# Windowed attention into a gated unit: one four-bank score tile against two two-bank tiles

## The chip, the cores and the metric

The kernel runs on one core of one Trainium2 chip. The metric is the device time of one execution in microseconds; the time before is the median of three executions. The profile is of one further execution, taken by the hardware profiler. Engine names are those of the profile: PE is TensorE, with PEld for its weight loads, DVE is VectorE, ACT is ScalarE, POOL is GpSimd, SP is SyncE.

## The reference

Eight batches of 576 positions go through an attention of 8 heads with head size 64, and its result through a gated unit of width 512. Heads 0 to 3 see the last 32 positions; heads 4 to 7 see every fourth of the last 128.

```python
def _attn_ref(q, k, v):                      # each (8, 8, 576, 64) fp32
    scores = 1.0 / np.sqrt(64) * np.matmul(q, k.transpose(0, 1, 3, 2))
    rel = pos[:, None] - pos[None, :]
    mask_plain = (rel >= 0) & (rel < 32)                         # heads 0-3
    mask_dil = (rel >= 0) & (rel < 128) & (rel % 4 == 0)         # heads 4-7
    scores = np.where(masks, scores, -1e9)
    attn = np.exp(scores - max(scores)); attn = attn / (sum(attn) + 1e-9)
    return np.matmul(attn, v)

def _moe_ref(x, w_val, conv_w, w_out):       # x: (8, 576, 512)
    gate_pre = sum over k of conv_w[k] * (x shifted by 4 - k positions)   # 5 taps, causal
    gate = 1.0 / (1.0 + np.exp(-gate_pre))
    return (gate * (x @ w_val)) @ w_out      # fp32 out
```

## The kernel before

The work is cut into 32 steps, four to a batch. A step does two heads: steps 0 and 1 of a batch have plain windows, steps 2 and 3 dilated ones. Each step is done in two halves (`hf` 0 and 1). The program order is written by hand and kept on every engine (`manual_schedule`); the framework adds the semaphores between engines, and a new tile of a pool waits until the readers of the tile whose place it takes are done.

PSUM has eight banks of 2 KiB in each partition. The kernel divides them among three pools:

```python
    ps_tr = ctx.enter_context(tc.tile_pool(name="ps_tr", bufs=2, space=PSUM))    # transposes: 2 x 1 bank
    ps_sc = ctx.enter_context(tc.tile_pool(name="ps_sc", bufs=1, space=PSUM))    # scores: 1 x 4 banks
    ps_moe = ctx.enter_context(tc.tile_pool(name="ps_moe", bufs=2, space=PSUM))  # gated unit: 2 x 1 bank
```

A half step of attention: six score matmuls into two banks of the score tile, one exponential over both, a multiply by the 0/1 mask, six products with V. The V operand has a column of ones, so that each product brings its sum of weights along. The products go into the first of the half's two banks, over the scores.

```python
    def scores(i, hf):
        if hf == 0:
            st[(i, "ps")] = ps_sc.tile([128, 4, 512], FP32, name="ps_sc")
        ps = st[(i, "ps")][:, 2 * hf:2 * hf + 2, :]
        for n in range(3):
            for sl in range(2):
                ...
                nc.tensor.matmul(out=o, lhsT=lhsT, rhs=rhs, start=True, stop=True)       # L386
        ...
        nc.scalar.activation(out=e3, in_=ps[:, :, 0:HB], func=AF.Exp, scale=scale)       # L389

    def apply_mask(i, hf):
        ...
        nc.vector.tensor_tensor(out=e3, in0=e3, in1=m, op=ALU.mult)                      # L398

    def attn_v(i, hf):
        et, ps = st[(i, "et")], st[(i, "ps")]
        ...                                                        # 6 of:
                nc.tensor.matmul(                                                        # L416
                    out=ps[:, 2 * hf, x * AVS:x * AVS + D + 1],
                    lhsT=et[:, (2 * hf + sl) * HB + col:(2 * hf + sl) * HB + col + 128],
                    rhs=rhs, start=True, stop=True)

    def normalize(i):                                              # both halves at once
        ...
        nc.vector.reciprocal(out=rec[0:R], in_=av[:, :, :, D])                           # L428
        ...
        nc.vector.tensor_tensor(                                                         # L433
            out=dst, in0=av[:, :, :, 0:D],
            in1=rec[0:R, :, :, None].to_broadcast([R, 2, 6, D]), op=ALU.mult)
```

`trans_main` (L312) and `trans_rest` (L345) transpose the queries and keys of the next group of heads into a `ps_tr` tile, from which ScalarE and VectorE copy them out (L322 to L358). `trans_x` (L445 to L460) transposes the normalized output into `xT`. The gated unit takes `ps_moe` tiles: `conv` (L484, read by a tanh at L492), `val` (L499, read by the gating multiply into `y_all` at L505) and `out_tile` (L514, copied out at L519 and stored). One step puts them in this order:

```python
        scores(i, 0)
        scores(i, 1)
        if i > 0:
            trans_x(i - 1)
            ...
        if g + 1 < 2 * B:
            ...            # trans_main(g + 1, "k"), or trans_main(g + 1, "q") and trans_rest(g + 1)
        ...
        apply_mask(i, 0)
        ...
        pop_dense(0.5)     # val or out_tile, as a budget allows
        pop_conv(i)
        apply_mask(i, 1)
        ...
        attn_v(i, 0)
        pop_conv(i + 0.5)
        ...
        attn_v(i, 1)
        normalize(i)
        ...                # the first three steps: warming matmuls on junk data (L576)
        pop_dense(1.5)
```

Of the kernel before, what the change touches and what calls it, by code (L numbers as in the profile page):

```python
# [7 lines left out]
FP32 = mybir.dt.float32  # L8
BF16 = mybir.dt.bfloat16
I32 = mybir.dt.int32  # L10
AF = mybir.ActivationFunctionType
ALU = mybir.AluOpType
PSUM = bass.MemoryType.PSUM
# [10 lines left out]
def kernel(  # L24
# [11 lines left out]
    nc = tc.nc  # L36
# [29 lines left out]
    gate_pool = ctx.enter_context(tc.tile_pool(name="gate", bufs=16))  # L66
    out_pool = ctx.enter_context(tc.tile_pool(name="osb", bufs=4))

    ps_tr = ctx.enter_context(tc.tile_pool(name="ps_tr", bufs=2, space=PSUM))
    ps_sc = ctx.enter_context(tc.tile_pool(name="ps_sc", bufs=1, space=PSUM))  # L70
    ps_moe = ctx.enter_context(tc.tile_pool(name="ps_moe", bufs=2, space=PSUM))

    ctx.enter_context(tc.manual_schedule())

# [23 lines left out]
    conv_diag = consts.tile([128, NCH, K, 128], BF16, name="conv_diag")  # L98
    w_val_b = consts.tile([128, NCH, Dm], BF16, name="w_val_b")
    w_out_b = consts.tile([128, NCH, Dm], BF16, name="w_out_b")  # L100


    grp_tiles = {}
# [171 lines left out]
            out=mb, in0=mb, in1=same[:, :, None].to_broadcast([128, 2, TR]), op=ALU.mult)  # L275

    def setup_conv_w():
        ps = ps_moe.tile([128, 512], FP32, name="ps_moe")
        for c in range(NCH):
            nc.tensor.transpose(  # L280
                out=ps[:, c * 8:c * 8 + K], in_=conv_nat[:, c * 128:(c + 1) * 128],
                identity=ident5[0:K, 0:K],
            )
        nc.scalar.copy(
            out=conv_w_sb, in_=ps[:, 0:NCH * 8].rearrange("p (c e) -> p c e", c=NCH)[:, :, 0:K])
# [15 lines left out]
    def trans_main(g, name, pairs=(0, 1)):  # L301

        dil = g % 2
        t = grp_tiles[g]
        ps = ps_tr.tile([128, 2, RM], BF16, name="ps_tr")
        for z in pairs:
            for m in range(4):
                if not dil:
                    src = t[name + "b"][:, m, 2 * z:2 * z + 2, :]
                else:  # L310
                    src = hi_bf16(t[name][:, 2 * z + m // 2, 128 * (m % 2):128 * (m % 2) + 128])
                nc.tensor.transpose(out=ps[:, z, TM * m:TM * m + TM], in_=src, identity=ident)  # L312
        z0, z1 = pairs[0], pairs[-1] + 1
        if name == "q":
            if not dil:
                if "qT" not in t:
                    t["qT"] = qt_pool.tile([128, 2, DIL, T], BF16, name="qT")
                qd, qs = t["qT"][:, z0:z1, :, 0:TM], ps[:, z0:z1, :].rearrange("p z (r t) -> p z r t", r=DIL)
                if g == 0:
                    nc.vector.tensor_copy(qd, qs)  # L320
                else:
                    nc.scalar.copy(out=qd, in_=qs)  # L322
            else:
                t["qA"] = qt_pool.tile([128, 2 * RM], BF16, name="qA")
                nc.scalar.copy(out=t["qA"], in_=ps.rearrange("p z n -> p (z n)"))
        else:
            if not dil:
                t["kT"] = kTs[(g // 2) % NKT]
                nc.scalar.copy(
                    out=t["kT"][:, z0:z1, KOFF:KOFF + RM].rearrange("p z (t r) -> p z t r", r=DIL),  # L330
                    in_=ps[:, z0:z1, :].rearrange("p z (r t) -> p z t r", r=DIL))
            else:
                t["kA"] = qt_pool.tile([128, 2 * RM], BF16, name="kA")
                t["kB"] = qt_pool.tile([128, 4, 64, 2], BF16, name="kB")
                nc.scalar.copy(out=t["kA"], in_=ps.rearrange("p z n -> p (z n)"))
                nc.scalar.copy(
                    out=t["kB"][:, :, 0:TM - TB, :],
                    in_=ps.rearrange("p z (h w t) -> p (z h) t w", h=2, w=2)[:, :, TB:TM, :])

    def trans_rest(g):  # L340
        dil = g % 2
        t = grp_tiles[g]
        ps = ps_tr.tile([128, 2, RM], BF16, name="ps_tr")
        for z in range(2):
            nc.tensor.transpose(  # L345
                out=ps[:, 0, TM * z:TM * z + TM],
                in_=hi_bf16(t["rest"][:, 128 * z:128 * z + 128]), identity=ident)
        pv = ps[:, 0, 0:256].rearrange("p (z n) -> p z n", z=2)
        if not dil:
            nc.vector.tensor_copy(t["kT"][:, :, KOFF + RM:KOFF + S], pv[:, :, 0:64])  # L350
            nc.vector.tensor_copy(
                t["qT"][:, :, :, TM:T], pv[:, :, 64:128].rearrange("p z (t r) -> p z r t", r=DIL))
        else:
            t["qB"] = qt_pool.tile([128, 4, 2, TR], BF16, name="qB")
            nc.vector.tensor_copy(
                t["kB"][:, :, TM - TB:64, :],
                pv[:, :, 0:64].rearrange("p w (h t) -> p h t w", h=4))
            nc.vector.tensor_copy(  # L358
                t["qB"], pv[:, :, 64:128].rearrange("p w (h t) -> p h w t", h=4))
# [3 lines left out]
    def scores(i, hf):  # L363
        b, c, dil, g, a = pair_info(i)
        t = grp_tiles[g]
        if hf == 0:
            st[(i, "ps")] = ps_sc.tile([128, 4, 512], FP32, name="ps_sc")
        ps = st[(i, "ps")][:, 2 * hf:2 * hf + 2, :]
        for n in range(3):
            for sl in range(2):  # L370
                p0 = sl * D
                if not dil:
                    m = 3 * hf + n
                    o = ps[:, sl, 96 * n:96 * n + 96]
                    lhsT = t["kT"][p0:p0 + D, a // 2, 96 * m:96 * m + 128]
                    rhs = t["qT"][p0:p0 + D, a // 2, :, 24 * m:24 * m + 24]
                elif n < 2:
                    x = TM * (2 * (a + hf) + n)
                    o = ps[:, sl, TM * n:TM * n + TM]
                    lhsT = t["kA"][p0:p0 + D, x:x + TM]  # L380
                    rhs = t["qA"][p0:p0 + D, x:x + TM]
                else:
                    o = ps[:, sl, 2 * TM:HB]
                    lhsT = t["kB"][p0:p0 + D, a + hf, :, :]
                    rhs = t["qB"][p0:p0 + D, a + hf, :, :]
                nc.tensor.matmul(out=o, lhsT=lhsT, rhs=rhs, start=True, stop=True)  # L386
        et = ets[i % NET]
        e3 = et[:, 2 * hf * HB:2 * (hf + 1) * HB].rearrange("p (h n) -> p h n", h=2)
        nc.scalar.activation(out=e3, in_=ps[:, :, 0:HB], func=AF.Exp, scale=scale)  # L389
        st[(i, "et")] = et  # L390
# [8 lines left out]

    def attn_v(i, hf):  # L400
        b, c, dil, g, a = pair_info(i)
        et, ps = st[(i, "et")], st[(i, "ps")]
        for n in range(3):
            for sl in range(2):
                if not dil:
# [2 lines left out]
                else:  # L408
# [5 lines left out]

                x = 3 * sl + n if dil else 2 * n + sl
                nc.tensor.matmul(  # L416
                    out=ps[:, 2 * hf, x * AVS:x * AVS + D + 1],
                    lhsT=et[:, (2 * hf + sl) * HB + col:(2 * hf + sl) * HB + col + 128],
                    rhs=rhs, start=True, stop=True)

    def normalize(i):
        b, c, dil, g, a = pair_info(i)
        R = 128 if dil else 96
        xn = st[(i, "xn")] = xn_pool.tile([128, 2, 3, 2, D], BF16, name="xn")
        av = st[(i, "ps")][0:R].rearrange("p (f s) c -> p f s c", f=2)[:, :, 0, 0:6 * AVS].rearrange(
            "p f (x e) -> p f x e", x=6)
        rec = rec_pool.tile([128, 2, 6], FP32, name="rec")
        nc.vector.reciprocal(out=rec[0:R], in_=av[:, :, :, D])  # L428
        if dil:
            dst = xn[0:R].rearrange("p z n h d -> p h (z n) d")  # L430
        else:
            dst = xn[0:R].rearrange("p z n h d -> p z (n h) d")
        nc.vector.tensor_tensor(  # L433
            out=dst, in0=av[:, :, :, 0:D],
            in1=rec[0:R, :, :, None].to_broadcast([R, 2, 6, D]), op=ALU.mult)

    def trans_x(i):
        b, c, dil, g, a = pair_info(i)
        xn = st[(i, "xn")]
        px = ps_tr.tile([128, 2, RM], BF16, name="ps_tr").rearrange("p z n -> p (z n)")  # L440
        ps = px[:, 0:S]
        pr = ps.rearrange("p (r t) -> p r t", r=DIL)
        if not dil:
# [21 lines left out]

    def conv(b, c, G):
        xt = xTs[b % NXT]
        ps = ps_moe.tile([128, 512], FP32, name="ps_moe")
        r0 = 2 * G
        pieces = []  # L470
        for m in range(K):
# [22 lines left out]

    def val(b, c, G):
        xt = xTs[b % NXT]
        ps = ps_moe.tile([128, 512], FP32, name="ps_moe")
        for mc in range(NCH):
            nc.tensor.matmul(  # L499
                out=ps[:, 0:HB],  # L500
# [8 lines left out]
        )  # L509

    def out_tile(n):
        ps = ps_moe.tile([128, 512], FP32, name="ps_moe")
        for c in range(NCH):
            nc.tensor.matmul(  # L514
                out=ps, lhsT=y_all[:, c, 128 * n:128 * n + 128], rhs=w_out_b[:, c, :],
# [40 lines left out]
    def pop_conv(i):  # L556
        if convs and convs[0][0] < i:
            run(convs.pop(0)[1])
# [13 lines left out]

    def warm(n):
        for _ in range(n):
            ps = ps_moe.tile([128, 512], FP32, name="ps_moe")
            nc.tensor.matmul(out=ps, lhsT=junk[:, 0:128], rhs=junk, start=True, stop=True)  # L576

    warm(8)
# [7 lines left out]
    for i in range(NP):  # L586
# [35 lines left out]
        if i < 3:  # L622
            warm(2)
        attn_v(i, 0)
        pop_conv(i + 0.5)
        if i < 3:
            warm(2)
        attn_v(i, 1)
        normalize(i)
        if i < 3:  # L630
            warm(3)
        pop_dense(1.5)
# [38 lines left out]
```

The softmax here doesn't subtract the row's maximum and nothing guards it: scores larger than these inputs give would overflow.

## Time and profile before

| | |
|---|---|
| time, median of 3 (lowest to highest) | 249.35 us (247.44 to 251.14) |
| span of the profiled execution | 247.9 us |
| mean granted TensorE clock | 0.95 |
| exponential (L389), 128x576 | 64 x 650 ns |
| mask multiply (L398), 128x576 | 64 x 477 to 499 ns |
| reciprocal (L428), 12 columns | 32 x 231 ns |
| normalizing multiply (L433), 768 columns | 32 x 955 ns |
| gating multiply (L505), 288 columns | 64 x 449 ns |
| copy of one transposed group (L322 to L335), 1024 columns | 1012 ns |
| copy into the convolution's input (L460), 576 columns | 32 x 458 ns |

The page's busy table gives each engine's busy time, its share of the span and its number of instructions. An engine that isn't full tells nothing by itself: what matters is for what it stands still. The view of waits lists, for each kind of instruction, how long its engine had been idle before it and which instruction's end released it. A timeline lists instructions by start and length, with that idle time in brackets. A name such as `L386` is a line of the kernel; `ps_sc<-qA,kA` is output and inputs.

### The profile page before, as it was taken

Reading aid. Unit: us, or ns where it says so; the run is one execution under the profiler, and the core shown is the slowest. Engines: PE = TensorE matmul, PEld = TensorE weight load, DVE = VectorE, ACT = ScalarE, POOL = GpSimd, SP = SyncE. Lnnn points to the kernel's source line nnn. Section 1 sums busy time; section 2 is a strip of 40 time slices with the busy share of each in tenths; the row PEclk is TensorE's granted clock in tenths of the full one; section 3 lists DMA queues with packets and bytes.
Section 4 is the critical chain, followed back from the end, with each engine's and each line's share of the span. In section 5 each row is a group of like instructions: output and inputs, shape, how many; then the busy total and the mean of one; then the engine's idle time right before and its main releaser. Section 6 shows DMA issues by size and latency. Waiting matters only on the chain.

```text
span 247.9 us, 5248 instructions
## 1 busy us (share of the span) xinstructions
PE 190.5 (77%) x2050; PEld 129.7 (52%) x2072; DVE 118.3 (48%) x284; ACT 123.4 (50%) x206; POOL 38.6 (16%) x87
## 2 busy tenths in 40 slices
PE   6495875978777788788887887778787878868992
PEld 2353543756555555565555655555565645556550
DVE  3535515455345545455545553555455543655330
ACT  3234324346654564655574556646573657443322
POOL 7005505000600024005100330006002000000000
PEclk9659598599999999999999999999999999999999
DMA  6969999642966398869275945599275123101415
GB/s 186 274 212 278 255 263 296 191 128 72 269 167 180 126 266 180 251 182 278 70 207 187 321 81 134 192 326 200 68 207 175 24 50 94 49 0 45 127 44 169
DMA packets 63186, 42.29 MB, mean 171 GB/s; under 512 B 31925, under 2 KB 58549, under 8 KB 63162
## 3 DMA queue, kind: packets, MB, share of 16 engines
q1 hardware_dynamic: 61280, 40.31, 58.5%
q0 software_dynamic: 1056, 1.05, 2.7%
q10 hardware_dynamic: 826, 0.60, 0.8%
q8 instruction: 16, 0.26, 0.4%
q14 instruction: 8, 0.07, 0.1%
HBM read 33.56 MB, written 9.44 MB: 173 GB/s over the span
## 4 chain that ended last, share of the span: by engine, by line
PE 53%; DVE 22%; ACT 9%; DMA 6%; issue 5%; SPq 2%; ACTq 0%
PE ps_moe L484 12%; PE ps_moe L514 11%; ACT et L389 7%; PE ps_sc L386 6%; DVE xn L433 6%; PE ps_sc L416 6%; PE ps_moe L499 6%; DVE et L398 5%; DMA qk_rest<-in_k_dram 4%; DVE y_all L505 4%; PE ps_tr L312 3%; PE ps_moe L576 3%; DVE xT L460 3%; PE ps_tr L445 2%; DMA k_nat<-in_k_dram 2%
## 5 line engine op out<-in xcount | busy, mean ns | idle before, releaser
L389 ACT ACTIVATE et<-ps_sc 128x576 bf16<-128x576 f32 x64 | 41.6, 650 | 46.7 <-PE ps_sc L386 46.2
L484 PE MATMUL ps_moe<-xT,conv_diag 128*128 128x288 bf16 (+1 forms) x384 | 51.1, 269 | 1.3 <-DVE y_all L505 0.7
L492 ACT ACTIVATE gate<-ps_moe 128x288 bf16<-128x288 f32 x64 | 26.1, 412 | 37.7 <-PE ps_moe L484 37.4
L499 PE MATMUL ps_moe<-xT,w_val_b 128*128 128x288 bf16 x256 | 40.4, 293 | 4.9 <-DVE y_all L505 4.6
L460 DVE COPY xT<-ps_tr 128x576 bf16<-128x576 bf16 x32 | 14.6, 458 | 54.3 <-PE ps_tr L458 32.4
L484 PEld LDWEIGHTS <-conv_diag 128*128 128x128 bf16 x384 | 32.5, 99 | 9.3 <-issue 2.6
L514 PE MATMUL ps_moe<-w_out_b,y_all 128*128 128x512 bf16 x124 | 33.6, 379 | 1.1
L505 DVE SCALAR_TENSOR_TENSOR y_all<-gate,ps_moe 128x288 bf16<-128x288 bf16 x64 | 27.7, 449 | 11.2 <-PE ps_moe L499 9.9
L519 ACT ACTIVATE osb<-ps_moe 128x512 f32<-128x512 f32 x36 | 21.5, 597 | 20.1 <-PE ps_moe L514 18.8
L499 PEld LDWEIGHTS <-w_val_b 128*128 128x128 bf16 x256 | 24.2, 100 | 13.7 <-issue 6.6
L433 DVE TENSOR_TENSOR xn<-ps_sc,rec 96x768 bf16<-96x768 f32 (+1 forms) x32 | 30.6, 955 | 1.1
L416 PEld LDWEIGHTS <-et 128*128 128x128 bf16 x384 | 21.6, 99 | 17.7 <-DVE et L398 12.6
L168 POOL CAST k_b<-k_nat 128x512 bf16<-128x512 f32 x14 | 9.3, 692 | 134.0 <-DMA k_nat<-in_k_dram 99.1
L428 DVE RECIPROCAL rec<-ps_sc 96x12 f32<-96x12 f32 (+1 forms) x32 | 7.4, 231 | 42.0 <-PE ps_sc L416 42.0
L386 PE MATMUL ps_sc<-qT,kT 64*128 64x96 bf16 x192 | 10.2, 212 | 15.8 <-ACT et L389 13.9
L386 PE MATMUL ps_sc<-qA,kA 64*128 64x128 bf16 x128 | 9.4, 224 | 14.8 <-ACT et L389 12.4
L514 PEld LDWEIGHTS <-y_all 128*128 128x128 bf16 x144 | 13.0, 97 | 11.9 <-issue 0.3
L386 PEld LDWEIGHTS <-kT 64*128 64x128 bf16 x192 | 5.9, 97 | 23.1 <-issue 19.5
L416 PE MATMUL ps_sc<-vP,et 128*128 128x65 bf16 x192 | 14.4, 200 | 4.1 <-DVE et L398 3.9
L386 PEld LDWEIGHTS <-kA 64*128 64x128 bf16 x128 | 5.4, 95 | 21.6 <-issue 16.5
L576 PE MATMUL ps_moe<-junk 128*128 128x512 bf16 x34 | 14.6, 534 | 2.0 <-DVE junk L196 1.5
L398 DVE TENSOR_TENSOR et<-et,mask_d 128x576 bf16<-128x576 bf16 x32 | 15.2, 499 | 0.0
(78 smaller groups left out, 207.1 us busy)
## 6 DMA issues: line engine op xcount, KB each, us to landing
k_nat<-in_k_dram SPq DMA_DIRECT2D x15, 512.0 KB, 5.7
q_nat<-in_q_dram SPq DMA_DIRECT2D x15, 512.0 KB, 5.8
vP<-in_v_dram SPq DMA_DIRECT2D x7, 768.0 KB, 7.8
v_st<-in_v_dram SPq DMA_DIRECT2D x8, 512.0 KB, 3.9
vB_st<-in_v_dram SPq DMA_DIRECT2D x8, 256.0 KB, 4.8
out_dram<-osb SPq DMA_DIRECT2D x8, 256.0 KB, 2.8
out_dram<-osb SPq DMA_DIRECT2D x8, 224.0 KB, 2.5
out_dram<-osb SPq DMA_DIRECT2D x8, 192.0 KB, 2.5
```

The lines of the kernel that those rows point to most:

```text
L386: nc.tensor.matmul(out=o, lhsT=lhsT, rhs=rhs, start=True, stop=True)
L389: nc.scalar.activation(out=e3, in_=ps[:, :, 0:HB], func=AF.Exp, scale=scale)
L398: nc.vector.tensor_tensor(out=e3, in0=e3, in1=m, op=ALU.mult)
L416: nc.tensor.matmul(out=ps[:, 2 * hf, x * AVS:x * AVS + D + 1], lhsT=et[:, (2 * hf + sl) * HB + col:(2 * hf + sl) * HB + col + 128], rhs=rh ...
L433: nc.vector.tensor_tensor(out=dst, in0=av[:, :, :, 0:D], in1=rec[0:R, :, :, None].to_broadcast([R, 2, 6, D]), op=ALU.mult)
L460: nc.vector.tensor_copy(xTs[b % NXT][:, c, :, 2:], pr)
L484: nc.tensor.matmul(out=ps[:, o * T:(o + n) * T], lhsT=conv_diag[:, c, K - 1 - m, :], rhs=xt[:, c, r:r + n, off:off + T], start=(idx == 0), ...
L492: nc.scalar.activation(out=gate, in_=ps[:, 0:HB], func=AF.Tanh, scale=0.5)
L499: nc.tensor.matmul(out=ps[:, 0:HB], lhsT=w_val_b[:, mc, c * 128:(c + 1) * 128], rhs=xt[:, mc, 2 * G:2 * G + 2, 2:], start=(mc == 0), stop= ...
L505: nc.vector.scalar_tensor_tensor(out=y_all[:, c, b * S + G * HB:b * S + (G + 1) * HB], in0=gates.pop((b, c, G)), scalar=1.0, in1=ps[:, 0:H ...
L514: nc.tensor.matmul(out=ps, lhsT=y_all[:, c, 128 * n:128 * n + 128], rhs=w_out_b[:, c, :], start=(c == 0), stop=(c == NCH - 1),)
L576: nc.tensor.matmul(out=ps, lhsT=junk[:, 0:128], rhs=junk, start=True, stop=True)
```

## The change

The score tile of four banks becomes two tiles of two banks, one to a half, from a pool of two. The normalization is done for each half by itself, the first directly after the first half's products. The pools of the transposes and of the gated unit become one pool of four single banks, which all their tiles take in turn. It is for letting a half go its way without the other, and for giving each single-bank tile a longer time until its bank is wanted again. The arithmetic is the same.

```diff
-    ps_tr = ctx.enter_context(tc.tile_pool(name="ps_tr", bufs=2, space=PSUM))
-    ps_sc = ctx.enter_context(tc.tile_pool(name="ps_sc", bufs=1, space=PSUM))
-    ps_moe = ctx.enter_context(tc.tile_pool(name="ps_moe", bufs=2, space=PSUM))
+    ps_sc = ctx.enter_context(tc.tile_pool(name="ps_sc", bufs=2, space=PSUM))
+    ps_one = ctx.enter_context(tc.tile_pool(name="ps_one", bufs=4, space=PSUM))
...
+    def bank():
+        return ps_one.tile([128, 512], FP32, name="ps_bank")
+
+    def bank_b():
+        return bank().bitcast(BF16).rearrange("p (z n) -> p z n", z=2)
...   (every ps_tr tile becomes bank_b(), every ps_moe tile becomes bank())
     def scores(i, hf):
-        if hf == 0:
-            st[(i, "ps")] = ps_sc.tile([128, 4, 512], FP32, name="ps_sc")
-        ps = st[(i, "ps")][:, 2 * hf:2 * hf + 2, :]
+        ps = st[(i, hf)] = ps_sc.tile([128, 2, 512], FP32, name="ps_sc")
...
     def attn_v(i, hf):
-        et, ps = st[(i, "et")], st[(i, "ps")]
+        et, ps = st[(i, "et")], st[(i, hf)]
...
-                    out=ps[:, 2 * hf, x * AVS:x * AVS + D + 1],
+                    out=ps[:, 0, x * AVS:x * AVS + D + 1],
...
-    def normalize(i):
+    def normalize(i, hf):
...
-        rec = rec_pool.tile([128, 2, 6], FP32, name="rec")
-        nc.vector.reciprocal(out=rec[0:R], in_=av[:, :, :, D])
+        av = st[(i, hf)][0:R, 0, 0:6 * AVS].rearrange("p (x e) -> p x e", x=6)
+        rec = rec_pool.tile([128, 6], FP32, name="rec")
+        nc.vector.reciprocal(out=rec[0:R], in_=av[:, :, D])
...
         nc.vector.tensor_tensor(
-            out=dst, in0=av[:, :, :, 0:D],
-            in1=rec[0:R, :, :, None].to_broadcast([R, 2, 6, D]), op=ALU.mult)
+            out=dst, in0=av[:, :, 0:D],
+            in1=rec[0:R, :, None].to_broadcast([R, 6, D]), op=ALU.mult)
...
         attn_v(i, 0)
+        normalize(i, 0)
         pop_conv(i + 0.5)
...
         attn_v(i, 1)
-        normalize(i)
+        normalize(i, 1)
```

More of the change, by code (lines that the diff above doesn't have):

```diff
@@ L277, in setup_conv_w @@
     def setup_conv_w():
-        ps = ps_moe.tile([128, 512], FP32, name="ps_moe")
+        ps = bank()
         for c in range(NCH):
@@ L304, in trans_main @@
         t = grp_tiles[g]
-        ps = ps_tr.tile([128, 2, RM], BF16, name="ps_tr")
+        ps = bank_b()
         for z in pairs:
@@ L342, in trans_rest @@
         t = grp_tiles[g]
-        ps = ps_tr.tile([128, 2, RM], BF16, name="ps_tr")
+        ps = bank_b()
         for z in range(2):
@@ L416, in attn_v @@
                 nc.tensor.matmul(
-                    out=ps[:, 2 * hf, x * AVS:x * AVS + D + 1],
+                    out=ps[:, 0, x * AVS:x * AVS + D + 1],
                     lhsT=et[:, (2 * hf + sl) * HB + col:(2 * hf + sl) * HB + col + 128],
                     rhs=rhs, start=True, stop=True)
-    def normalize(i):
+    def normalize(i, hf):
         b, c, dil, g, a = pair_info(i)
         R = 128 if dil else 96
-        xn = st[(i, "xn")] = xn_pool.tile([128, 2, 3, 2, D], BF16, name="xn")
-        av = st[(i, "ps")][0:R].rearrange("p (f s) c -> p f s c", f=2)[:, :, 0, 0:6 * AVS].rearrange(
-            "p f (x e) -> p f x e", x=6)
-        rec = rec_pool.tile([128, 2, 6], FP32, name="rec")
-        nc.vector.reciprocal(out=rec[0:R], in_=av[:, :, :, D])
+        if hf == 0:
+            st[(i, "xn")] = xn_pool.tile([128, 2, 3, 2, D], BF16, name="xn")
+        xn = st[(i, "xn")]
+        av = st[(i, hf)][0:R, 0, 0:6 * AVS].rearrange("p (x e) -> p x e", x=6)
+        rec = rec_pool.tile([128, 6], FP32, name="rec")
+        nc.vector.reciprocal(out=rec[0:R], in_=av[:, :, D])
         if dil:
-            dst = xn[0:R].rearrange("p z n h d -> p h (z n) d")
+            dst = xn[0:R, :, :, hf, :].rearrange("p z n d -> p (z n) d")
         else:
-            dst = xn[0:R].rearrange("p z n h d -> p z (n h) d")
+            dst = xn[0:R, hf, :, :, :].rearrange("p n h d -> p (n h) d")
         nc.vector.tensor_tensor(
-            out=dst, in0=av[:, :, :, 0:D],
-            in1=rec[0:R, :, :, None].to_broadcast([R, 2, 6, D]), op=ALU.mult)
+            out=dst, in0=av[:, :, 0:D],
+            in1=rec[0:R, :, None].to_broadcast([R, 6, D]), op=ALU.mult)
     def trans_x(i):
@@ L439, in trans_x @@
         xn = st[(i, "xn")]
-        px = ps_tr.tile([128, 2, RM], BF16, name="ps_tr").rearrange("p z n -> p (z n)")
+        px = bank_b().rearrange("p z n -> p (z n)")
         ps = px[:, 0:S]
@@ L467, in conv @@
         xt = xTs[b % NXT]
-        ps = ps_moe.tile([128, 512], FP32, name="ps_moe")
+        ps = bank()
         r0 = 2 * G
@@ L496, in val @@
         xt = xTs[b % NXT]
-        ps = ps_moe.tile([128, 512], FP32, name="ps_moe")
+        ps = bank()
         for mc in range(NCH):
@@ L511, in out_tile @@
     def out_tile(n):
-        ps = ps_moe.tile([128, 512], FP32, name="ps_moe")
+        ps = bank()
         for c in range(NCH):
@@ L574, in warm @@
         for _ in range(n):
-            ps = ps_moe.tile([128, 512], FP32, name="ps_moe")
+            ps = bank()
             nc.tensor.matmul(out=ps, lhsT=junk[:, 0:128], rhs=junk, start=True, stop=True)
```

## The prediction

> **What bounds the kernel now.** I read the page's busy table first: no engine is full.
>
> ```profile
> PE 190.5 (77%) x2050; PEld 129.7 (52%) x2072; DVE 118.3 (48%) x284; ACT 123.4 (50%) x206; POOL 38.6 (16%) x87
> ```
>
> TensorE has most to do, and works 77% of the span. The slices and the windows split the span in four: start to 11 us (first loads and transposes), 11 to 40 us (first four attention steps, DMA engines full: share 1.02, granted clock 0.76), 40 to 227 us (the other 28 of 32 steps, DMA share 0.59, clock 0.98), and a tail to 248 us. In the long stage TensorE is busy 147.7 of 187 us, so it idles 39.3 us. The waits of TensorE within 40 to 227 us say for what (columns: total us, times, longest):
>
> ```profile
> PE ps_sc L386 <- ACT et L389: 23.4, 28, 1.3
> PE ps_moe L499 <- DVE y_all L505: 4.6, 7, 0.7
> PE ps_sc L416 <- DVE et L398: 4.5, 13, 0.7
> PE ps_sc L386 <- DVE xn L433: 3.5, 7, 1.4
> ```
>
> These are 36.0 of the 39.3 us. The first is one wait per step, 28 in 28 steps: the score matmuls wait for the exponential. The timeline of one step shows which half:
>
> ```profile
> 117.10 0.96 DVE L433 TENSOR_TENSOR xn<-ps_sc,rec 128x768 bf16<-128x768 f32 x1
> 117.98 0.81 DVE L505 SCALAR_TENSOR_TENSOR y_all<-gate,ps_moe 128x288 bf16<-128x288 bf16 x2
> ...
> 118.12 0.29 PE L386 MATMUL ps_sc<-qA,kA 64*128 64x128 bf16 x4 [0.34 <-DVE xn L433]
> ...
> 118.46 0.65 ACT L389 ACTIVATE et<-ps_sc 128x576 bf16<-128x576 f32 x1 [1.41 <-PE ps_sc L386]
> 119.16 0.29 PE L386 MATMUL ps_sc<-qA,kA 64*128 64x128 bf16 x4 [0.74 <-ACT et L389]
> ...
> 120.43 0.27 PE L345 MATMUL ps_tr<-ident,qk_rest 128*128 128x128 bf16 x2
> ...
> 121.08 0.82 DVE L398 TENSOR_TENSOR et<-et,mask_d 128x576 bf16<-128x576 bf16 x2
> ```
>
> The first half of the scores starts at 118.12, when the normalization of the step before has ended (118.06). The second half starts only at 119.16, when the first half's exponential (118.46 to 119.11) is done. It has no use for that result: it writes banks 2 and 3 of the score tile, and the exponential reads banks 0 and 1. The built instruction stream holds a wait on ScalarE at exactly that matmul, so it comes from both halves being one tile.
>
> **What the skill says.** The Trainium skill, "PSUM — Partial Sum Buffer", section Terms, gives eight banks. Both kernels use all eight, before as 2+4+2 and after as 2x2+4, so the change buys no space and only regroups. "Perfetto Trace Analysis", section Optimization Strategy, says that a gap repeating on the engine that should be saturated can mean too few PSUM buffers for the next tile. The 28 equal waits are such a gap, though the cause here is the size of the tile. The same page, section Optimizing Scalar/DVE Operations, says that splitting instructions may help where Vector isn't saturated but causes bubbles, and that a VectorE access to PSUM has a fixed cost near 125 ns, about twice that as latency. The trace agrees: VectorE is busy 48%, and the reciprocal of only 12 columns takes 231 ns.
>
> **The change part by part.**
>
> *The exponential wait goes.* In the changed kernel's built stream the first matmul of the second half waits on VectorE and TensorE, not on ScalarE. All of 23.4 us in the long stage leaves TensorE's path (0.84 us a step).
>
> *The normalization is split.* The first half's scores now need only the first half's normalization, which is issued before the second convolution and the second attention product, so it is done in time. The second half's scores need a shorter one. Size: the multiply takes 955 ns for 768 columns and y_all, also from PSUM, 449 ns for 288, so a column costs (955-449)/480 = 1.05 ns and the fixed part is about 145 ns. A half is then 145 + 384 x 1.05 = 550 ns. The reciprocal stays near 225 ns, as it is nearly all fixed. Each step on VectorE goes from 231+955 = 1186 to 2 x (225+550) = 1550 ns: 0.36 us more, 11.6 us over 32 steps (118 to 130 us busy). After the last attention product the wait is 0.8 us where it was 1.2, with over 1 us of dense matmuls to cover it. Of 3.5 us I count 2.8 gone.
>
> *The rotation of four.* A step takes two or three transpose tiles and about five others. In the shared rotation each waits for the reader of the tile four allocations back, before for two back in its own pool. So the L499 wait for y_all (4.6 us) mostly goes, I count 3.7. The transposes of the rest at L345 wait some 0.2 us for the xT copy in 13 steps (2.9 us in the weight loads' waits, under issue); I count 2.5 gone. The long readers are the 1.0 us copies of kA and qA plus 0.49 us for kB. Their bank comes up again two convolutions or so later, by which time they are done or nearly so.
>
> Sum of what goes: 23.4+2.8+3.7+2.5 = 32.4 us.
>
> *What comes.* From timelines of several steps, TensorE's throughput in one: scores 2 x 0.24, transposes 0.32 + 0.45 (+0.12), convolutions 2 x 0.62, attention 2 x 0.24, dense work about 2.0, in all 5.0 us. Let scores start at 0. TensorE then reaches the attention product at about 2.0 without dense work in between, 2.5 with one val, 2.8 with one output tile. Its last weights overlap the other half's columns, so it needs both masks. ScalarE: exponentials 0.3 to 0.95 and 0.95 to 1.65, or up to 2.2 where an output copy (0.60 us) is ahead. VectorE: xT copy 1.0 to 1.45; where there are rest copies, these to 2.0; mask 0.4; a y_all 0.4 in val steps; mask 0.4. The second mask ends between 2.6 and 3.3. So the attention product waits 0.2 to 0.7, I take 0.45 us a step, where L416 <- L398 now has 4.5/28 = 0.16. That gives back 0.29 x 28 = 8.1 us.
>
> Long stage: 32.4 - 8.1 = 24.3 us. Start and first four steps: four exponential waits of 0.74 us and a shorter start (L345 waits 3.2 us for a bank), but here DMA is full and the warming matmuls fill some gaps: 3 us. Tail: waits of 1.4 us for the two ps_moe banks: 1 us, while the last stores stay. In all 28 us: 249.35 - 28 = 221 us. I say 222, as sums of waits seldom come off the span whole.
>
> **Rivals.**
>
> *The wait moves whole to the masks.* Exponentials, masks, attention are a chain that was started early while TensorE stood still. For it: VectorE gets 0.36 us more a step, and in steps with four vals it has about 4.9 us of work in 5.5. Against it: between scores and attention TensorE has 2.0 to 2.8 us of other work. If the wait were 0.8 us a step instead of 0.45, 10 us more return: 222 + 10 = 232 us.
>
> *DMA becomes the bound.* For it: 0.59 of the DMA engines are busy over the long stage, and a step one sixth shorter makes it 0.7; loads queue behind stores on SyncE. Against it: no TensorE wait on a DMA is named there, and the loads are issued about four steps ahead. It would make some 230 us.
>
> *The shared rotation stalls.* A transpose tile behind a late output copy holds back work that had banks of its own. Order and copy lengths speak against it, as above; a 0.2 us stall a step would cost 6 us.
>
> *The clock.* "TensorE: Matmul & The Clock Gate", section HAM oscillation, says idle gaps over about 3.4 us throttle the array. The trace has half clock in three stretches before 49 us and full clock after, with TensorE gaps of 1.4 us at most. Fewer gaps should shorten these stretches, for 2 to 4 us more gain (218 us).
>
> **Range and chances.** The removed waits are measured, the returned ones are estimated. With no new wait, 221 - 8 = 213; with a full mask rival, 232. Slower would need new waits of 28 us, which no view supports; within 2% needs 23 us of them.
>
> **What would show it.** Right: no L386 <- ACT wait; VectorE near 130 us busy, multiply near 550 ns, x64; L416 <- mask grown to 10 to 15 us; L499 <- y_all near zero; TensorE busy about 85%; period of a step 5.6 to 5.8 us instead of 6.6. Wrong: a large wait of transposes or convolutions for a ScalarE copy (rotation), TensorE waits on DMA, or mask waits above 20 us.

## The result and the profile after

The changed kernel takes 202.51 us (median of four, 201.45 to 204.23) where the kernel before takes 248.58 us beside it (247.44 to 251.14). The ratio is 0.814, with a 95% interval from 0.805 to 0.823. That is a gain of 46 us; 27 us were predicted, and the time lies below the 213 us that stood for the case without any new wait. Executions of one kernel in this study spread over 1 to 3%, so differences of a few us between two kernels below are read from phases of the trace as well as from medians.

The busy table of the page after:

```profile
PE 177.1 (88%) x2072; PEld 123.7 (61%) x2072; DVE 129.3 (64%) x348; ACT 115.8 (57%) x206; POOL 39.3 (20%) x87
```

TensorE's busy time fell too, from 190.5 to 177.1 us, though it does the same matmuls (22 of them left no record in the trace before, so the fall is rather larger); part of the miss lies there. The waits of TensorE in steps 4 to 31 (33.9 to 182.7 us of the span; columns: total us, times, longest) are all there are:

```profile
PE ps_sc L419 <- DVE et L401: 6.9, 19, 0.6
PE ps_sc L419 <- ACT et L392: 2.7, 3, 1.9
PE ps_sc L389 <- DVE xn L437: 0.6, 2, 0.4
```

The exponential's wait before the scores is gone, and so is every wait of the gated unit for a bank. What is left, 10.2 us where there were 36.0, stands nearly all before the attention product, for masks and exponentials. One step of the timeline after:

```profile
106.80 0.43 PE L389 MATMUL ps_sc<-qT,kT 64*128 64x96 bf16 x12
107.14 1.19 ACT L392 ACTIVATE et<-ps_sc 128x576 bf16<-128x576 f32 x2 [1.49 <-PE ps_sc L389]
107.16 0.43 PE L449 MATMUL ps_bank<-ident,xn 96*128 96x96 bf16 x6
...
107.87 0.28 PE L350 MATMUL ps_bank<-ident,qk_rest 128*128 128x128 bf16 x2
...
108.52 0.45 DVE L401 TENSOR_TENSOR et<-et,mask_p 128x576 bf16<-128x576 bf16 x1
...
109.25 0.45 DVE L401 TENSOR_TENSOR et<-et,mask_p 128x576 bf16<-128x576 bf16 x1
...
109.76 0.20 PE L419 MATMUL ps_sc<-vP,et 128*128 128x65 bf16 x1 [0.34 <-DVE et L401]
```

All twelve score matmuls run through, and the transposes follow at 107.16, 0.36 us after the first of them. Before, the same stretch took 1.28 us, from 118.12 to the first transpose:

```profile
119.40 0.26 PE L452 MATMUL ps_tr<-perm,xn 96*128 96x96 bf16 x2
```

After, the first half's sixth attention matmul, whose weights overlap the second half, waits for the second mask (109.25 to 109.70).

Cut at the first score matmul of each step and at the last attention product, the profiled spans divide so (us):

| | before | after | gain | predicted |
|---|---|---|---|---|
| start, to the first scores | 11.2 | 10.1 | 1.1 | 3 with the next row |
| steps 0 to 3 | 31.3 | 23.8 | 7.5 | |
| steps 4 to 31 | 184.1 | 149.0 | 35.1 | 24.3 |
| tail | 21.3 | 18.7 | 2.7 | 1 |
| span | 247.9 | 201.5 | 46.4 | 28 |

Steps 4 to 30 by phase, from the start of one kind of matmul to the start of the next on TensorE (mean us per step):

| phase | before | after |
|---|---|---|
| scores to transposes | 1.386 | 0.391 |
| transposes to first attention product | 2.135 | 2.108 |
| first product to second convolution | 0.490 | 0.576 |
| second convolution to second product | 0.624 | 0.624 |
| second product to dense work | 0.211 | 0.191 |
| dense work to next scores | 1.812 | 1.503 |
| period | 6.659 | 5.393 |

### The profile page after: what moved, and what is told of

The parts are those of the page before. It is cut to its first block, busy times and chain, and to the rows that moved or that the text cites. A ratio compares the mean times of both kernels' runs of the same rounds, so it can differ in the third digit from the quotient of the medians.

```text
span 201.5 us, 5330 instructions
## 1 busy us (share of the span) xinstructions
PE 177.1 (88%) x2072; PEld 123.7 (61%) x2072; DVE 129.3 (64%) x348; ACT 115.8 (57%) x206; POOL 39.3 (20%) x87
## 4 chain that ended last, share of the span: by engine, by line
PE 59%; DMA 15%; DVE 12%; ACT 6%; issue 3%; SPq 3%; ACTq 0%
PE ps_bank L503 13%; PE ps_bank L518 12%; PE ps_bank L488 10%; DVE et L401 7%; PE ps_sc L419 6%; DMA qk_rest<-in_k_dram 5%; ACT et L392 5%; PE ps_bank L317 5%; PE ps_sc L389 4%; DMA out_dram<-osb 4%; DMA k_nat<-in_k_dram 4%; PE ps_bank L580 3%; DVE y_all L509 2%; PE ps_bank L449 2%; DMA q_nat<-in_q_dram 2%
## 5 line engine op out<-in xcount | busy, mean ns | idle before, releaser
L488 PE MATMUL ps_bank<-xT,conv_diag 128*128 128x288 bf16 (+1 forms) x384 | 50.2, 266 | 0.0
L496 ACT ACTIVATE gate<-ps_bank 128x288 bf16<-128x288 f32 x64 | 26.6, 423 | 27.3 <-PE ps_bank L488 26.7
L503 PE MATMUL ps_bank<-xT,w_val_b 128*128 128x288 bf16 x256 | 38.3, 290 | 0.0
L437 DVE TENSOR_TENSOR xn<-ps_sc,rec 96x384 bf16<-96x384 f32 (+1 forms) x64 | 35.6, 556 | 2.2
L419 PEld LDWEIGHTS <-et 128*128 128x128 bf16 x384 | 21.3, 99 | 22.6 <-DVE et L401 19.0
L518 PE MATMUL ps_bank<-w_out_b,y_all 128*128 128x512 bf16 x144 | 35.0, 379 | 0.0
L523 ACT ACTIVATE osb<-ps_bank 128x512 f32<-128x512 f32 x36 | 21.6, 599 | 21.9 <-PE ps_bank L518 13.7
L509 DVE SCALAR_TENSOR_TENSOR y_all<-gate,ps_bank 128x288 bf16<-128x288 bf16 x64 | 27.4, 449 | 8.8 <-PE ps_bank L503 8.0
L464 DVE COPY xT<-ps_bank 128x576 bf16<-128x576 bf16 x32 | 14.7, 458 | 25.2 <-PE ps_bank L462 18.5
L432 DVE RECIPROCAL rec<-ps_sc 96x6 f32<-96x6 f32 (+1 forms) x64 | 12.4, 194 | 17.0 <-PE ps_sc L419 16.1
L401 DVE TENSOR_TENSOR et<-et,mask_p 128x576 bf16<-128x576 bf16 x32 | 15.9, 508 | 3.6 <-ACT et L392 3.2
L580 PE MATMUL ps_bank<-junk 128*128 128x512 bf16 x36 | 13.5, 494 | 2.2 <-DVE junk L201 1.5
```

The costliest lines, as they stand in the source:

```text
L419: nc.tensor.matmul(out=ps[:, 0, x * AVS:x * AVS + D + 1], lhsT=et[:, (2 * hf + sl) * HB + col:(2 * hf + sl) * HB + col + 128], rhs=rhs, st ...
L437: nc.vector.tensor_tensor(out=dst, in0=av[:, :, 0:D], in1=rec[0:R, :, None].to_broadcast([R, 6, D]), op=ALU.mult)
L464: nc.vector.tensor_copy(xTs[b % NXT][:, c, :, 2:], pr)
L488: nc.tensor.matmul(out=ps[:, o * T:(o + n) * T], lhsT=conv_diag[:, c, K - 1 - m, :], rhs=xt[:, c, r:r + n, off:off + T], start=(idx == 0), ...
L496: nc.scalar.activation(out=gate, in_=ps[:, 0:HB], func=AF.Tanh, scale=0.5)
L503: nc.tensor.matmul(out=ps[:, 0:HB], lhsT=w_val_b[:, mc, c * 128:(c + 1) * 128], rhs=xt[:, mc, 2 * G:2 * G + 2, 2:], start=(mc == 0), stop= ...
```

## The experiments

The theory to test: TensorE sets the pace, and the gain is its removed stops, most at the score tile. Rivals for the unpredicted part: the shared rotation is worth far more than its listed waits; the early steps gain from the array's clock (23.9 us at half clock before, 10.2 us after, by the trace's clock record, not counting the idle end); or the early normalization matters by itself.

### Only the scores split

```diff
-    ps_one = ctx.enter_context(tc.tile_pool(name="ps_one", bufs=4, space=PSUM))
+    ps_tr = ctx.enter_context(tc.tile_pool(name="ps_tr", bufs=2, space=PSUM))
+    ps_moe = ctx.enter_context(tc.tile_pool(name="ps_moe", bufs=2, space=PSUM))
```

> The kernel after, but transposes and gated unit keep their own pools of two banks each, as before; only the scores are split in two tiles, with a normalization to each half. If the exponential wait and what each stop costs TensorE carry the gain, nearly all of it is here: 207 to 213 us, scores phase of a step 0.4 us as after, with the waits for xT and y_all (2.9 and some 4.6 us) back. If the shared rotation carries 10 us or more, 218 us or above.

212.49 us (209.18 to 212.82) against 247.98 us before: 35 us of gain, within the 207 to 213 us of the first theory. The profiled execution is the fastest of the four (209.18 us), so by the spans of the traces the gain is larger, 40 us. Steps 0 to 3 take 22.6 us, so the split alone brings all that the change brings there. Scores to transposes take 0.388 us a step, as after. The start (11.2 us) and the tail (20.9 us) stay nearly as they were before, so their 3.8 us of gain belong to the rotation. TensorE's waits in this kernel hold the gated unit's bank wait in small:

```profile
PE ps_sc L420 <- DVE et L402: 10.0, 23, 1.1
PE ps_tr L351 <- DVE qT L326: 3.1, 1, 3.1
PE ps_moe L504 <- DVE y_all L510: 1.7, 7, 0.3
```

### Only the shared rotation

```diff
-    ps_tr = ctx.enter_context(tc.tile_pool(name="ps_tr", bufs=2, space=PSUM))
     ps_sc = ctx.enter_context(tc.tile_pool(name="ps_sc", bufs=1, space=PSUM))
-    ps_moe = ctx.enter_context(tc.tile_pool(name="ps_moe", bufs=2, space=PSUM))
+    ps_one = ctx.enter_context(tc.tile_pool(name="ps_one", bufs=4, space=PSUM))
```

> The kernel before with only the four shared banks; one four-bank score tile and one normalization as before. If the rotation is worth just the waits on y_all and xT that it removes (about 4.6 + 2.9 + 1.4 in the tail, partly taken up by the next wait), 241 to 245 us, with the exponential wait of 0.84 us a step still there. If it carries a large part, 236 us or below.

232.83 us (232.43 to 234.72), ratio 0.943 (0.935 to 0.950): 15 us, where I had expected 3 to 7. Scores to transposes are unchanged at 1.383 us and the exponential's wait is all there:

```profile
PE ps_sc L391 <- ACT et L394: 26.4, 32, 1.3
PE ps_sc L421 <- DVE et L403: 7.3, 16, 1.6
PE ps_sc L391 <- DVE xn L438: 5.6, 10, 1.4
```

By place the gain is 1.7 us in the start, 1.8 in steps 0 to 3, 11.1 in steps 4 to 31 and 2.7 in the tail. Within a step it is 0.19 us from transposes to attention and 0.21 us in the dense work. The rest's transposes show how: from the group's transposes to the rest's took 0.71 us before and takes 0.45 us here, 0.26 us less, where the idle time listed there was about 0.22. The two parts alone bring 35 and 15 us by the medians and 40 and 17 by the traces, both together 46, so they overlap by 4 to 11 us. Within a step the overlap has two places: before the attention product the rotation's 0.19 us is nearly gone when both are in (2.108 us), as masks are waited for there, and in the dense work each alone brings 0.20 us and both bring 0.31.

### Both normalizations at the end

```diff
         attn_v(i, 0)
-        normalize(i, 0)
         pop_conv(i + 0.5)
 ...
         attn_v(i, 1)
+        normalize(i, 0)
         normalize(i, 1)
```

> The kernel after, with both halves normalized only after the second attention product. The first theory expects little, 203 to 206 us: two reciprocals and multiplies are 1.5 us, which the dense work at the end of a step (about 1.5 us) nearly covers, and only the tile split matters. If normalizing the first half early matters by itself, 209 us or more, and score matmuls wait for the multiply by 0.2 us a step or more.

202.07 us (198.66 to 203.98), and score matmuls waited for the multiply only 0.6 us in all. With two tiles each half has its own reciprocal and multiply; doing the first half's early is worth nothing that shows here.

### The kernel before, transposes between the score halves

```diff
         scores(i, 0)
-        scores(i, 1)
         if i > 0:
             trans_x(i - 1)
 ...
                 trans_rest(g + 1)
+        scores(i, 1)
```

> The kernel before, same tiles and banks, only the order changed: the transposes of a step (0.8 to 0.9 us of TensorE work) stand between its two score halves, where TensorE stood idle 0.84 us. If the idle time at that place is what the change was paid for, most of it returns without any new tile: 224 to 232 us, with the exponential wait near 0.1 us a step. If the gain came from PSUM banks or the clock, it stays above 243 us.

231.06 us (229.72 to 232.24), ratio 0.934 (0.925 to 0.943). Nearly half of what splitting the tile brings comes by order alone, with the tiles and banks of before. The waits:

```profile
PE ps_sc L416 <- ACT et L389: 6.2, 11, 0.8
PE ps_sc L386 <- DVE xn L433: 5.3, 10, 1.3
PE ps_sc L416 <- DVE et L398: 5.0, 19, 0.7
PE ps_moe L499 <- DVE y_all L505: 4.8, 7, 0.7
...
PE ps_sc L386 <- ACT et L389: 1.9, 7, 0.5
```

The wait before the scores fell from 26.4 to 1.9 us, but the second exponential now starts later, and the attention product waits 6.2 us for it. The other waits of before stay. So the stop at that place is what costs, and an order that only hides it moves part of it down the chain.

### The kernel before, stops filled in the first steps

```diff
         scores(i, 0)
+        if i < 7:
+            warm(3)
         scores(i, 1)
```

> The kernel before with three more junk matmuls between the two score halves in the first seven steps only, where TensorE stands idle for the exponential; no wait is removed. If half clock in the early steps (23.9 us of it before, 10.2 us after) carries several us of the gain, keeping the array busy there brings the clock up sooner and this takes 241 to 245 us, with less than 12 us of half clock. If the clock matters little, 247 to 251 us.

247.41 us (244.89 to 250.1), ratio 0.997 (0.994 to 1.000). The trace has 3.4 us of half clock where the kernel before has 23.9, and steps 0 to 3 take 31.1 us, as before. In steps 1 to 3 the two halves of the scores start 1.04 us apart, as before, so there the junk fits into the stop; in step 0 it costs 0.6 us. It may have taken some of what the clock gave, but no several us are in it, in this kernel that stops every step.

### The kernel after without warming matmuls in the steps

```diff
-        if i < 3:
-            warm(2)        # four such places, warm(3) in the last
```

> The kernel after without the junk matmuls of the first three steps (the nine at the start stay). If the first steps are paced by TensorE, they shorten by up to 6 us, unless the clock drops to half for longer, which gives some of it back: 198 to 204 us. If the loads pace the first steps, as the prediction had it for the kernel before, there is no change in steps 0 to 3 beyond 1 us: 201 to 204 us, with new waits for loads.

200.53 us (199.17 to 203.18). Here the clock stays at half for 17.1 us on end, from 10.6 us on, and TensorE has 27 matmuls less to do; steps 0 to 3 take 23.1 us against 23.8 after. The small difference is two larger ones. Up to its second attention product, step 0 is 2.6 us shorter (3.9 against 6.5 us from the first score matmul), without nine junk matmuls. From there to the second attention product of step 3 it is 1.9 us longer (18.7 against 16.8 us), with 18 junk matmuls less. That leaves the clock as the likely cause: the six matmuls of a convolution take nearly twice as long in that stretch as after it.

```profile
19.50 1.39 PE L488 MATMUL ps_bank<-xT,conv_diag 128*128 128x288 bf16 x6
...
31.70 0.79 PE L488 MATMUL ps_bank<-xT,conv_diag 128*128 128x288 bf16 x6
```

So once the score tile is split, TensorE's work and its clock both count in the first steps, and here they offset each other. The wait for loads is no longer than after (2.3 us, once).

### Padding behind each half of the exponentials

```diff
-    ets = [consts.tile([128, 4 * HB + 96], BF16, name=f"et{i}") for i in range(NET)]
+    EH = 2 * HB + 96
+    ets = [consts.tile([128, 2 * EH], BF16, name=f"et{i}") for i in range(NET)]
 ...
-                    lhsT=et[:, (2 * hf + sl) * HB + col:(2 * hf + sl) * HB + col + 128],
+                    lhsT=et[:, hf * EH + sl * HB + col:hf * EH + sl * HB + col + 128],
```

> The kernel after, with 96 columns of padding behind each half of the exponentials' tile, so that the last weights of the first half no longer overlap the second half and the first attention product needs only its own mask. If that overlap is what makes the product wait for the second mask, the phase from first attention product to second convolution falls from 0.58 to 0.50 us and the whole to 198 to 201 us. If the first mask is the one that is late, 202 us as before.

204.65 us (203.39 to 207.5), not faster. The overlap was what the product waited for: from first product to second convolution fell from 0.58 to 0.20 us, more than expected. But from transposes to first product it rose by as much, from 2.11 to 2.50 us. A new wait stands there, seen once at its worst in this timeline:

```profile
68.58 0.45 SPq L116 DMA_DIRECT2D k_nat<-in_k_dram  x1
...
71.83 3.64 SPq L133 DMA_DIRECT2D qk_rest<-in_q_dram  x4
...
76.61 1.19 SPq L530 DMA_DIRECT2D out_dram<-osb  x2
...
82.22 0.60 ACT L524 ACTIVATE osb<-ps_bank 128x512 f32<-128x512 f32 x1 [7.72 <-DMA out_dram<-osb]
82.71 1.19 ACT L393 ACTIVATE et<-ps_sc 128x576 bf16<-128x576 f32 x2
83.39 1.24 DVE L402 TENSOR_TENSOR et<-et,mask_p 128x576 bf16<-128x576 bf16 x2 [7.44 <-ACT et L393]
...
83.90 0.29 PE L420 MATMUL ps_sc<-vP,et 128*128 128x65 bf16 x2 [7.39 <-ACT et L393]
```

An output copy on ScalarE waits 7.7 us for an earlier store to leave one of four output buffers, and the exponentials, masks and products stand behind it. The stores are issued on SyncE behind the loads of later groups: this one at 76.61, after loads that begin at 68.58, and it landed at 82.1. In all, ScalarE waited 17.4 us for stores here; in the kernel after it was 2.6 us.

### The first mask before other VectorE work

As padded, and:

```diff
                 trans_main(g + 1, "q")
-                trans_rest(g + 1)
-        if i < NCH:
-            make_conv_diag(i)
         apply_mask(i, 0)
+        if g + 1 < 2 * B and a != 0:
+            trans_rest(g + 1)
 ...
         apply_mask(i, 1)
+        if i < NCH:
+            make_conv_diag(i)
```

> As the padded version, and VectorE does the first mask before the rest copies, and the building of the convolution's diagonals after the second mask. TensorE's order is kept. If VectorE's queue ahead of the masks is what remains of the attention product's waits (9.6 us in 28 steps, and more in the first four), 194 to 198 us. If the exponential itself is late, 199 us or more.

202.00 us (199.17 to 204.57), not under 199. In its profile steps 0 to 3 take 20.1 us against 22.5 in the padded version. Of these 2.4 us, 1.1 are in step 0, which starts 1.3 us later here and waits less for the same load (1.1 us for 2.0). Steps 1 to 3 take 13.9 us against 15.2, and in the two versions with ten output buffers below 14.2 against 15.2. So VectorE's queue ahead of the masks (the diagonals alone are 0.8 us a step) held the products back by about 1 us in all there. The gain went again into one wait of 7.4 us on the same chain of store, output copy and exponential; a split of that wait by cause beyond this was not tried.

### Ten output buffers

One edit on the mask-first version, on the padded version and on the kernel after:

```diff
-    out_pool = ctx.enter_context(tc.tile_pool(name="osb", bufs=4))
+    out_pool = ctx.enter_context(tc.tile_pool(name="osb", bufs=10))
```

> The mask-first version with ten output buffers in place of four. In its trace ScalarE stood 11.7 us before output copies for stores that were queued behind loads, once for 7.4 us, and the exponential behind it. If the buffers are what runs out, these waits are gone and it takes 190 to 195 us, under the kernel after. If the stores themselves or the loads are the limit, 198 us or more, with TensorE waiting for loads instead.

> The padded version with ten output buffers. In the padded version ScalarE stood 17.4 us for stores, so the padding's own worth was hidden. If padding is worth the 0.08 us a step between first product and second convolution plus part of the waits ahead, this takes 195 to 200 us; if padding is worth nothing, it equals the kernel after with ten buffers.

> The kernel after with ten output buffers and no other edit: the reference for the two others. In its trace ScalarE stood only 2.6 us for stores, so 199 to 202 us; were the buffers already its limit, 197 us or less.

Mask first 198.13 us (193.74 to 199.76), padded 197.55 (196.92 to 199.94), after with ten buffers 198.06 (196.64 to 199.58). The last two are 0.796 (0.790 to 0.802) and 0.799 (0.792 to 0.806) of the kernel before. ScalarE no longer waits for stores in any of the three, so the four buffers were what ran out, and all three have medians under the kernel after; but the interval of that kernel's ratio (0.805 to 0.823) still touches that of the same kernel with ten buffers. For the kernel after alone I had expected a little less gain, and for mask first 190 to 195 us, which it missed: there TensorE waits 7.4 us for loaded keys. Between the three no difference can be told. TensorE's waits in the padded one show what took the place of the waits for masks:

```profile
PE ps_bank L318 <- DMA k_nat<-in_k_dram: 5.9, 4, 2.3
PE ps_bank L318 <- POOL k_b L174: 2.8, 5, 1.4
...
PE ps_sc L420 <- DVE et L402: 2.5, 6, 1.0
```

The waits for masks fell to 2.5 us, and transposes now wait for loaded keys and for GpSimd's cast of them. In its long stage TensorE is busy 94% and the DMA engines 0.85 (0.77 in the kernel after). Loads are what it waits for next; no run here makes them faster.

## Why the prediction was wrong

The direction and the mechanism held: the exponential's wait left the path, the bank waits left it, mask waits took a part back, and nothing else became the bound. The sizes of the multiply (556 ns, predicted 550) and of VectorE's busy time (129 us, predicted 130) held too; the reciprocal did not, 194 ns where 225 were predicted as "nearly all fixed". What failed is the sum, in these terms.

**The exponential's wait, 23.4 us, was mis-sized.** The step "all of 23.4 us in the long stage leaves TensorE's path (0.84 us a step)" took the listed idle time for the cost of the stop. Scores to transposes lost 0.995 us a step, 27.9 us in 28 steps, 4.5 more than listed. The rest is in the score matmuls' own busy time: they overlap less when they stop halfway. Before and then after, in the groups by form (busy us, mean ns, then idle before):

```profile
L386 PE MATMUL ps_sc<-qT,kT 64*128 64x96 bf16 x192 | 10.2, 212 | 15.8 <-ACT et L389 13.9 <-DVE xn L433 1.9
L386 PE MATMUL ps_sc<-qA,kA 64*128 64x128 bf16 x128 | 9.4, 224 | 14.8 <-ACT et L389 12.4 <-DVE xn L433 2.3
L386 PE MATMUL ps_sc<-qB,kB 64*128 64x32 bf16 x64 | 6.1, 179 | 0.0
```

```profile
L389 PE MATMUL ps_sc<-qT,kT 64*128 64x96 bf16 x192 | 7.2, 206 | 0.6 <-DVE xn L437 0.6
L389 PE MATMUL ps_sc<-qA,kA 64*128 64x128 bf16 x128 | 7.0, 218 | 0.0
L389 PE MATMUL ps_sc<-qB,kB 64*128 64x32 bf16 x64 | 5.1, 175 | 0.0
```

The matmuls are of nearly the same length in both. Taken together (the last two groups overlap in time) the 384 are busy 20.1 us before and 14.5 us after, and in steps 4 to 31 17.2 and 12.4 us: 4.8 us, or 0.17 us a step, that no list of idle time shows. The waits had been read from the right view, but they are not all that a stop costs. The ends of matmuls in the trace are modelled, so the split of the 0.995 us between idle and busy is rough; the start-to-start time is not.

**The waits before the attention product, 8.1 us given back, were set too high.** They rose from 4.5 to 9.6 us (6.9 for masks, 2.7 for exponentials), by 5.1. My 0.45 us a step was 0.34.

**The normalization and the rotation were set too low.** Dense work to next scores lost 0.31 us a step, 8.7 us, where I counted 6.5 for normalization and y_all; the rest's transposes lost 0.26 us in 13 steps, 3.4 us for my 2.5. The four terms, 4.5 + 3.0 + 2.2 + 0.9 = 10.6 us, are nearly all of the 10.8 us between 24.3 and 35.1. Stops at a bank, too, cost more than they list: the rotation alone took 11.1 us off steps 4 to 31, where the waits for y_all and xT that it removes were listed with 4.6 + 2.9 us, and the 256 matmuls of `val` (L499 before) are busy 38.1 us instead of 40.4.

**The start and the first steps, 3 us, were mis-sized by 5.6.** The step that failed is "here DMA is full and the warming matmuls fill some gaps". The DMA engines were full (1.02), yet the loads were ahead of the need: steps 0 to 3 went from 31.3 to 23.8 us with one new wait for a load of 2.3 us. The share of busy DMA engines says how much is moved, not that somebody waits for it; the view of waits had no TensorE wait on a load there, and I gave the share more weight. Most of the 7.5 us is the stop at the scores: the split alone brought 8.6 us there, the other order alone 4.9, the rotation alone 1.8. What the clock has in it is not settled: half clock cost nothing that shows in the kernel that stops, and probably some 2 us in steps 1 to 3 of the one that does not.

**The tail** gave 2.7 us for my 1, nearly all of it by the rotation: the rotation alone brought 2.7 us there, the split alone 0.4.

Of the rivals, the waits did not move whole to the masks, the shared rotation did not stall (one wait of 0.7 us for a ScalarE copy), and the kernel before ran no faster with less half clock. Nor do idle gaps of over 3.4 us, which the prediction took as what throttles the array, account for the trace before: the clock fell to half at 24.9 and at 42.0 us, and no gap of TensorE from 11.2 us on is over 1.4 us. The DMA rival came up only beyond the kernel after, near 198 us, through the output buffers first and the loads then. Last, the discount from 221 to 222, since sums of waits seldom come off the span whole, went the wrong way here: more came off than the sum.

## What to carry to other kernels

Where TensorE works in a fixed order and stops once a step, compare the start-to-start time of the phase with that of the same work run through; the listed idle time (0.84 us here) is less than what the stop costs (1.0 us). Two halves that use different banks of one tile may still wait for each other; give each its own tile, and see in the trace that the wait is gone. When the stops are gone, look at once for what has little slack left: here output buffers that wait for stores queued behind loads.

## What the runs showed of the hardware

- The reciprocal from PSUM is not all fixed cost: 231 ns for 12 columns (in two rows of 6) and 194 ns for 6, about 6 ns a column, where the multiply's 955 ns for 768 columns and 556 ns for 384 make about 1 ns a column.
- Half clock on TensorE cost little where the array stops for others, and probably more where it runs through. In the kernel before, 3.4 us of it instead of 23.9 changed the time by 0.3% (ratio 0.994 to 1.000), with junk matmuls in the stops. In the kernel after, the stretch from the second attention product of step 0 to that of step 3 took 16.8 us mostly at full clock, and 18.7 us mostly at half clock though with 18 junk matmuls less.
